# Attention followed by a mixture of experts on one core: the denominators' sums shared between two engines, the seventh batch's routing placed earlier and cut in four

## The chip, the cores and the metric

The kernel runs on one core of a Trainium2 chip. Five engines work side by side: TensorE (PE, matrix products; its weight loads are listed apart as PEld), VectorE (DVE), ScalarE (ACT), GpSimd (POOL) and SyncE (SP), which issues most of the loads. Each engine takes its own instructions strictly in order. The metric is the device time of one execution in microseconds (us).

## The reference

```python
# attention: 8 batches, 12 heads, 448 tokens, 64 wide, float32
scores = cap * tanh(q @ k.T / sqrt(64) / cap)
attn = exp(scores - max);  attn /= sum(attn) + 1e-9
x = (attn @ v), laid out as (3584 tokens, 768)
# experts: 8 of them, 768 -> 1024 -> 768
logits = x @ w_gate + modality_bias[modality_id]
e_idx = argmax(logits);  gate_w = softmax(logits)[e_idx]
out[mask] = gate_w[mask] * (relu(x[mask] @ w1[e]) @ w2[e])   # mask: e_idx == e
```

Each token goes to one expert, so the kernel has to know the expert of every token before it can gather the rows of an expert.

## The kernel before

**Attention.** A group `g` is one pair of heads of one batch: 48 groups (`NG`), six to a batch, and one more turn of the loop (`g = 48`) that finishes the last. In group `g` PE makes the scores of group `g` in four steps (L451; steps 0 and 1 first, then the work of step 1, then steps 2 and 3, then the work of step 3). ACT takes the tanh (`th`, L453) and the exp (`pt`, and `sh` for the step that both heads share, L455). While it does so, PE weighs the values of group `g - 1`: `weigh_own` (L460) with the six parts `pt`, `weigh_shared` (L465) with `sh`, both into the PSUM tile `xT`, of which there is one buffer; DVE copies it out (L588). DVE also prepares the next group's keys and queries as a rounded part `hi` and a rest `lo` (`prep`, L439 and L440), and adds the six `pt` parts into two (`tot`, L557 and L558), for the denominators.

**Sums.** For every three groups (a half batch, `h`), `sums` makes four parts on PE into the tile `glog` (L475). Parts 0 and 1 sum `tot` over the keys, part 2 sums `sh`, part 3 multiplies the unnormalised values `xT` by the gate's weights; `gl` copies the result (L479). Parts 0 and 1 run in one group, parts 2 and 3 in the next. The half batch 13, the last one of the seventh batch (`SOON`), has its four parts in one group, 43. `by_token` turns the result round (`lt`, L487), `logits` divides (L492, L495), `rows_out` transposes the values themselves and scales them (L505, L506) into `xs`, and `store` sends these to device memory (`xd`, L515).

**Routing.** When a batch has its logits, `route` picks the expert of each token on DVE (L210 to L234). At the next group's step 3 it ranks the tokens with two small products on PE (L238, L240), computes rows on DVE, and scatters four lists with indirect DMAs from POOL's queue (`mapd`, L264).

**The first expert slot begins before the last batch is routed.** After the seventh batch, `early_slot` (L284 to L300) counts the tokens of each expert so far and picks one that surely fills a slot of 384 rows. Its result `emeta` gives the address of the rows: POOL loads the list (`mt`, L681) and gathers the rows (`xg`, L688), and SP loads the expert's first weights (`raw`, 18 tiles for the slot of which 6 are `w1`; L88 is the helper of all loads on SP) once DVE's small copy `when` (L610) has handed over the expert's number. `SPLITS` and `MOVES` say at which group and step a weight tile is split into a rounded part `ah` and a rest `al` (L704 on ACT, L705 on DVE) and at which one 128 columns of the gathered rows are transposed (`ptr`, L725) and split in the same way (`x`, L732 to L735).

**Experts.** `ffn1` makes eight blocks of hidden units (`ph`, L752 to L756, 18 products each), `ffn2` the output (`py`, L781). Between the blocks of the first slot stand the last batch's remaining sums, logits, routing and the plan of all later slots. From there on PE is busy with products without a pause worth the name until the last slots.

**What sets the order.** `pin` holds an instruction to the order in which the program is written, on its engine. What is not pinned is placed by a scheduler; `rows_out` on PE, the DVE adds and the SP loads are pinned, and so are the gathers; the stores, the scatters and the small steps of the routing are not.

## Time and profile before

| | |
|---|---|
| median of 3 runs | 955.42 us (949.41 to 956.46) |
| the profiled execution's own time | 955.9 us, span 954.0 us |
| PE busy | 906.7 us, 95% of the span |
| ACT busy | 558.8 us, 59% |
| DVE busy | 549.2 us, 58% |
| POOL busy | 129.7 us, 14% |
| attention, with what of the first slot lies in it | up to 420 us |
| one batch in the middle of the attention | 48.38 us |

A timeline row is: start, duration, engine, line, operation, output and inputs, how many instructions are merged in the row, and in brackets the idle time of the engine ahead of it with what ended that. A group row is: line, engine, operation, shapes and count, then the busy time with the mean of one in ns, then the idle time ahead of it. A window row is: stretch, its length, then for PE, PEld, DVE, ACT and POOL the busy time with the count of instructions, then the TensorE clock granted (1.00 is full speed), the mean busy share of the DMA engines and GB/s. An 'x12' on PE in fp32 is six products, since each takes two passes.

### The profile page before, as it was taken

The page shows a single profiled execution, that of the slowest core. Times are in us where ns is not written, and L with a number is a line of the kernel's source. Part 1 is how long each engine was busy: PE and PEld are TensorE (multiplying, and loading weights), DVE is VectorE, ACT ScalarE, POOL GpSimd, SP SyncE. Part 2 cuts the span into 40 slices and gives each one's busy share as a digit, 9 for nine tenths or more (in the row PEclk, how much of TensorE's full clock was granted, in tenths as well). Part 3 has the DMA queues.
Part 4 walks back from the last instruction along what each step waited for, and adds up shares of the span by engine and source line. Part 5 has one row for each costly group of instructions (what it writes and reads, how often), then busy time and mean ns, then how long its engine had stood idle before and what let it go on. Part 6 is the DMA issues. An engine that isn't in the chain of part 4 may idle for free. (4 is left out here: it accounts for less than half of the span.)

```text
span 954.0 us, 14504 instructions
## 1 busy us (share of the span) xinstructions
PE 906.7 (95%) x5360; PEld 699.8 (73%) x5360; DVE 549.2 (58%) x941; ACT 558.8 (59%) x759; POOL 129.7 (14%) x145
## 2 busy tenths in 40 slices
PE   8999999999999998489999999999999999999986
PEld 3444545454545445258899999999999999988986
DVE  4777777777777778276544443433434444427752
ACT  5998888888888887451544443433434444435551
POOL 2002020202020202102410202020200102010000
PEclk9999999999999999699999999999999999999998
DMA  3433444453436345632773535353454646237560
GB/s 120 119 101 110 134 116 134 115 133 116 127 122 124 125 124 97 197 132 81 259 245 127 197 134 185 126 176 150 161 204 144 221 127 217 81 130 252 197 203 6
DMA packets 47178, 140.01 MB, mean 147 GB/s; under 512 B 8686, under 2 KB 9198, under 8 KB 47088
## 3 DMA queue, kind: packets, MB, share of 16 engines
q1 hardware_dynamic: 38000, 105.78, 36.0%
q0 software_dynamic: 8944, 33.10, 10.4%
q8 instruction: 47, 0.77, 0.4%
q14 instruction: 43, 0.35, 0.1%
q10 hardware_dynamic: 144, 0.00, 0.0%
HBM read 117.35 MB, written 22.69 MB: 147 GB/s over the span
## 5 line engine op out<-in xcount | busy, mean ns | idle before, releaser
L453 ACT ACTIVATE th<-sc,isc 128x896 f32<-128x896 f32 x192 | 168.5, 906 | 68.1 <-PE sc L451 67.9
L756 PE MATMUL ph<-x,al 128*128 128x384 f32 (+2 forms) x528 | 167.7, 318 | 0.0
L781 PE MATMUL py<-bh,hh 128*128 128x384 f32 x464 | 158.7, 343 | 1.5 <-ACT hh L762 1.5
L781 PE MATMUL py<-bh,hl 128*128 128x384 f32 x464 | 156.5, 337 | 0.0
L781 PE MATMUL py<-bl,hh 128*128 128x384 f32 x464 | 156.2, 337 | 0.0
L455 ACT ACTIVATE pt<-th,cabs 128x896 f32<-128x896 f32 x144 | 149.5, 1043 | 2.7
L752 PE MATMUL ph<-x,ah 128*128 128x384 f32 x384 | 129.8, 338 | 4.0 <-DVE x L735 2.6
L753 PE MATMUL ph<-x,ah 128*128 128x384 f32 x384 | 129.4, 337 | 0.0
L460 PE MATMUL xT<-pt,va 128*64 128x448 f32 x576 | 122.0, 560 | 7.3 <-DVE xT L588 7.0
L705 DVE TENSOR_TENSOR bl<-raw,bh 128x768 fp32r<-128x768 f32 x88 | 81.2, 955 | 51.9 <-ACT bh L704 51.6
L704 ACT CAST bh<-raw 128x768 fp32r<-128x768 f32 x88 | 70.3, 840 | 60.1 <-DMA raw<-in_w_dram 54.8
L756 PEld LDWEIGHTS ph<-x,al 128*128 128x128 f32 x528 | 101.5, 192 | 0.0
L705 DVE TENSOR_TENSOR al<-raw,ah 128x1024 fp32r<-128x1024 f32 x66 | 78.8, 1222 | 27.7 <-ACT ah L704 27.4
L762 ACT ACTIVATE hh<-ph 128x384 fp32r<-128x384 f32 x64 | 30.5, 488 | 109.4 <-PE ph L756 104.9
L451 PEld LDWEIGHTS sc<-hi 64*128 64x128 f32 (+1 forms) x336 | 36.9, 189 | 76.3 <-ACT th L453 24.7
L786 ACT ACTIVATE ot<-py,mt 128x384 f32<-128x384 f32 x58 | 33.7, 581 | 98.3 <-PE py L781 49.7
L451 PE MATMUL sc<-hi 64*128 64x448 f32 (+1 forms) x336 | 88.0, 452 | 1.5 <-ACT th L453 0.8
L460 PEld LDWEIGHTS xT<-pt,va 128*64 128x64 f32 x576 | 38.0, 139 | 69.6 <-issue 46.4
L781 PEld LDWEIGHTS py<-bh,hh 128*128 128x128 f32 x464 | 87.1, 188 | 1.9 <-ACT hh L762 1.9
L781 PEld LDWEIGHTS py<-bl,hh 128*128 128x128 f32 x464 | 87.2, 188 | 0.3 <-DVE bl L705 0.2
L781 PEld LDWEIGHTS py<-bh,hl 128*128 128x128 f32 x464 | 87.2, 188 | 0.1
L791 POOL DMA_INDIRECT out_dram<-ot,mt x29 | 32.2, 1109 | 390.5 <-ACT ot L786 310.7
(160 smaller groups left out, 1352.9 us busy)
## 6 DMA issues: line engine op xcount, KB each, us to landing
raw<-in_w_dram SPq DMA_DIRECT2D x66, 512.0 KB, 4.7
raw<-in_w_dram SPq DMA_DIRECT2D x88, 384.0 KB, 4.8
kq<-in_kq_dram SPq DMA_DIRECT2D x47, 480.0 KB, 3.5
va<-in_v_dram SPq DMA_DIRECT2D x48, 256.0 KB, 2.7
xd<-xs POOLq DMA_DIRECT2D x16, 672.0 KB, 5.3
mapd<-pay,pos POOLq DMA_INDIRECT x32, 5.5
xg<-xd,mt POOLq DMA_INDIRECT x30, 5.9
out_dram<-ot,mt POOLq DMA_INDIRECT x29, 4.8
```

Of the source, the lines that this page charges most:

```text
L451: pin(pe.matmul(sc[:, j, :S], k[rows, ks], q[rows, KC2:], start=i == 0, stop=i == 2))
L453: nc.scalar.activation(th[:, :n], sc[:, :n, :S], AF.Tanh, scale=self.isc)
L455: nc.scalar.activation(dst, th[:, :n] if step < KU else th[:, 0], AF.Exp, scale=self.cabs)
L460: pin(pe.matmul(xT[j * D : (j + 1) * D, :S], va[:, u * D : (u + 1) * D], pt[:, u], start=u < 2, stop=False))
L704: a = self.nc.scalar.copy(hi, raw)
L705: b = self.nc.vector.tensor_tensor(lo, raw, hi, op=ALU.subtract)
L752: nc.tensor.matmul(ph[:, :w], hi[:, fs], self.x[:, k, 0, :w], start=first, stop=False)
L753: nc.tensor.matmul(ph[:, :w], hi[:, fs], self.x[:, k, 1, :w], start=False, stop=False)
L756: nc.tensor.matmul(ph[:, :w], lo[:, fs], self.x[:, k, 0, :w], start=False, stop=last)
L781: nc.tensor.matmul(py[:, :HALF], self.h[a][:, f, rows], self.w2s[f][c][:, cs], start=i == 0, stop=i == 3 * FC - 1,)
L786: nc.scalar.mul(ot[:, cs], py[:, :HALF], mt[:, t, 1:2])
L791: nc.gpsimd.indirect_dma_start(self.out, bass.IndirectOffsetOnAxis(ap=mt.bitcast(I32)[:, t, 0:1], axis=0), ot, None, bounds_check=NT - 1, ...
```

## The change

- `sums` loses its part for `sh`. Instead POOL adds `sh` into `tot`: two adds of 64 partitions x 448 for each group (`add`), after DVE's two. The part with the gate's weights comes first now (part 0, in the first of the two groups), and the two parts on `tot` follow in the next. For `g = 47` and `48` the adds of DVE and POOL are put off until after the attention's loop.
- `route` pauses at three places instead of one. For the first six batches its four parts run in four groups. For the last two batches three parts run at once. The fourth of the seventh batch stands, with `early_slot` behind it, at step 1 of group 44 instead of step 3, ahead of the next `prep`.
- `weigh_own` is written ahead of `prep` and the adds.
- The seventh batch's last store goes out on SP's queue, in program order, ahead of the loads of group 47; POOL's queue issued it before.
- All six `w1` tiles of the first slot are loaded at once: four into the staging buffers, two into the buffers of `kq`, made wider for that.
- Splits and transposes of the first slot stand later: nothing of it in group 46; the first two tiles are rounded by DVE (`busy`) instead of ACT.
- In the first slot the rest `bl` of the first four `w2` tiles is subtracted by POOL instead of DVE.
- Two constants become smaller: `pick`, and `ones`, which the warming products at the start read 384 columns wide instead of 512.

```diff
+        yield
...
+        yield
...
-        kq = pool.tile([128, QK], F32, name="kq")
+        kq = pool.tile([128, FF], F32, name="kq")[:, :QK]
...
+            def add(tot, ppt, psh):
+                pin(nc.vector.tensor_tensor(tot, ppt[:, 0:2], ppt[:, 2:4], op=ALU.add))
+                pin(nc.vector.tensor_tensor(tot, tot, ppt[:, 4:6], op=ALU.add))
+                for j in range(2):
+                    rows = slice(j * KR, (j + 1) * KR)
+                    nc.gpsimd.tensor_tensor(tot[rows, j], tot[rows, j], psh[rows], op=ALU.add)
             def weigh_shared(xT, sh, va):
...
                 for t in range(HB):
-                    xs_, tot, sh = kept[h * HB + t]
-                    w = self.pick[:, part] if part < 3 else self.wgt[:, (h * HB + t) % NP]
-                    rhs = (tot[:, 0], tot[:, 1], sh, xs_)[part]
-                    pin(pe.matmul(self.glog[t * GW : (t + 1) * GW, :S], w, rhs, start=part == 0, stop=part == 3))
+                    xs_, tot = kept[h * HB + t]
+                    w = self.pick[:, part - 1] if part else self.wgt[:, (h * HB + t) % NP]
+                    rhs = (xs_, tot[:, 0], tot[:, 1])[part]
+                    pin(pe.matmul(self.glog[t * GW : (t + 1) * GW, :S], w, rhs, start=part == 0, stop=part == 2))
...
-            def store(h, xs):
+            def store(h, xs, queue=nc.gpsimd):
                 b, h0 = divmod(h, NH)
-                nc.gpsimd.dma_start(
+                keep = pin if queue is nc.sync else (lambda inst: inst)
+                keep(queue.dma_start(
                     self.xd[b * S : (b + 1) * S, h0 * HB * 128 : (h0 + 1) * HB * 128].rearrange("(p c) f -> p c f", c=C),
                     xs,
-                )
-            SPLITS = {
-                (NG - 2, 3): (0,),
-                (NG - 1, 1): (1,),
-                (NG - 1, 3): (2,),
-                (NG, 0): (3,),
-                (NG, 2): (4,),
-                (NG, 3): (5,),
-            }
-            MOVES = {(NG - 2, 3): (0,), (NG - 1, 3): (1,), (NG, 1): (2, 3), (NG, 2): (4,), (NG, 3): (5,)}
+                ))
+            SPLITS = {(NG - 1, 1): (0,), (NG - 1, 2): (1,), (NG - 1, 3): (2,), (NG, 0): (3,), (NG, 2): (4,), (NG, 3): (5,)}
+            MOVES = {(NG - 1, 3): (0,), (NG, 1): (1, 2), (NG, 2): (3, 4), (NG, 3): (5,)}
...
             fetch(1)
-            kept, lgs, recs, routing, raws = {}, {}, {}, {}, []
+            adds = []
+            kept, lgs, recs, routing = {}, {}, {}, []
             for g in range(NG + 1):
...
                     if step == 1:
+                        if g:
+                            ppt, psh, pva = pend
+                            xT = ps_x.tile([128, 512], F32, name="xT")
+                            weigh_own(xT, ppt, pva)
+                        if g == NP * (B - 1) + 2:
+                            for way in routing:
+                                next(way, None)
+                            meta = self.early_slot(self.cpool, self.ps_r)
                         if g + 1 < NG:
...
                         if g:
-                            ppt, psh, pva = pend
                             tot = xp.tile([128, 2, S], F32, name="tot", bufs=HB + 2)
-                            pin(nc.vector.tensor_tensor(tot, ppt[:, 0:2], ppt[:, 2:4], op=ALU.add))
-                            pin(nc.vector.tensor_tensor(tot, tot, ppt[:, 4:6], op=ALU.add))
-                            xT = ps_x.tile([128, 512], F32, name="xT")
-                            weigh_own(xT, ppt, pva)
+                            adds.append((tot, ppt, psh))
+                            if g < NG - 1:
+                                add(*adds.pop())
...
                             h, r = divmod(g - HB - 1, HB)
-                            parts = {0: (0, 1), 1: (2, 3), 2: ()}[r] if h != SOON else () if r else range(4)
+                            parts = {0: (0,), 1: (1, 2), 2: ()}[r] if h != SOON else () if r else range(3)
                             for part in parts:
                                 sums(h, part)
-                            if 3 in parts:
+                            if 2 in parts:
                                 gl = copy_sums()
                     if step == 3:
-                        if g in routing:
-                            next(routing.pop(g), None)
+                        for way in routing:
+                            next(way, None)
                         if g == 3:
...
                             self.gate_bias()
-                        if g == NP * (B - 1) + 2:
-                            meta = self.early_slot(self.cpool, self.ps_r)
                         for i, p in enumerate(ROWS.get(g, ())):
...
                             if t == HB - 1:
-                                store(h, xs)
+                                store(h, xs, nc.sync if h == SOON else nc.gpsimd)
                         if g:
...
                             pin(nc.vector.tensor_copy(xs_, xT[:, :S]))
-                            kept[g - 1] = xs_, tot, psh
+                            kept[g - 1] = xs_, tot
                         fetch(g + 2)
...
                                 way = self.route(b, lgs[b], rp, self.ps_r)
-                                next(way)
-                                routing[g + 1] = way
+                                for _ in range(1 if b < B - 2 else 3):
+                                    next(way)
+                                routing = [way]
                     for k in SPLITS.get((g, step), ()):
-                        self.split_w(raws[k], self.w1s[k], pin=True)
-                        if len(raws) < KC:
-                            raws.append(self.load_raw(e, self.w1, len(raws), FF))
+                        self.split_w(raws[k], self.w1s[k], pin=True, busy=k < 2)
                     for k in MOVES.get((g, step), ()):
-                        early_ps = {2: (ps_s, "sc"), 3: (ps_s, "sc"), 5: (self.ps_r, "small")}
-                        self.transpose(k, *early_ps.get(k, (ps_v, "tp")), busy=k < 2, pin=True)
+                        early_ps = {0: (ps_v, "tp"), 3: (ps_v, "tp"), 4: (self.ps_r, "small")}
+                        self.transpose(k, *early_ps.get(k, (ps_s, "sc")), busy=k < 1, pin=True)
                     if (g, step) == (NG - 2, 1):
...
                         e = self.expert(when, 0)
-                        raws = [self.load_raw(e, self.w1, k, FF) for k in range(self.nstage)]
+                        raws = []
+                        for k in range(KC):
+                            raws.append(self.load_raw(e, self.w1, k, FF, None if k < self.nstage else qk.tile([128, FF], F32, name="kq")))
                 if g < NG:
...
                     self.gather(maps, known=NT - S)
+            for pair in adds:
+                add(*pair)
             self.raws = [self.load_raw(e, self.w2, k, DM) for k in range(self.nstage)]
...
             def last_sums():
-                for part in range(4):
+                for part in range(3):
                     sums(NH * B - 1, part, self.ps_y, "py")
...
                 self.way = self.route(B - 1, lgs[B - 1], rp, self.ps_r)
-                next(self.way)
+                for _ in range(3):
+                    next(self.way)
...
-    def load_raw(self, e, src, k, width):
-        raw = self.stg.tile([128, FF], F32, name="raw")
+    def load_raw(self, e, src, k, width, dst=None):
+        raw = self.stg.tile([128, FF], F32, name="raw") if dst is None else dst
         self.load(
...
-    def split_w(self, raw, dst, pin=False):
+    def split_w(self, raw, dst, pin=False, busy=False, minus=None):
         hi, lo = dst
-        a = self.nc.scalar.copy(hi, raw)
-        b = self.nc.vector.tensor_tensor(lo, raw, hi, op=ALU.subtract)
-        if pin:
-            self.pin(a)
-            self.pin(b)
+        keep = self.pin if pin else (lambda inst: inst)
+        keep((self.nc.vector.tensor_copy if busy else self.nc.scalar.copy)(hi, raw))
+        (keep if minus is None else (lambda inst: inst))((minus or self.nc.vector).tensor_tensor(lo, raw, hi, op=ALU.subtract))
...
-    def load_w2(self, e, raws=(), ks=range(FC)):
+    def load_w2(self, e, raws=(), ks=range(FC), minus=None):
         for k in ks:
             raw = raws[k] if k < len(raws) else self.load_raw(e, self.w2, k, DM)
-            self.split_w(raw, self.w2s[k], pin=bool(raws))
+            self.split_w(raw, self.w2s[k], pin=bool(raws), minus=minus)
...
         if n == TW:
-            self.load_w2(cur[0], raws, range(FC // 2 if between else FC))
+            self.load_w2(cur[0], raws, range(FC // 2 if between else FC), self.nc.gpsimd if between else None)
         nxt = ahead() if ahead and not between else None
```

POOL and SP around the gather of the first slot. On POOL before, from the seventh batch's scatter on (`emeta` is the early slot's address, `mt` its list, `xd<-xs` a store, `xg` the gather):

```order
L264 DMA mapd<-pay,pos 31104x2 x4
L94 TENSOR_LOAD emeta
L94 ISA x2
L681 ISA
L681 DMA mt<-mapd 128x6
L255 IOTA pay 112x4
L515 DMA xd<-xs 448x1x384
L688 DMA xg<-xd,mt 128x768 x3
```

On POOL now, from the same scatter on:

```order
L265 DMA mapd<-pay,pos 31104x2 x4
L94 TENSOR_LOAD emeta
L94 ISA x2
L693 ISA
L693 DMA mt<-mapd 128x6
L256 IOTA pay 112x4
L470 TENSOR_TENSOR tot<-tot,sh 64x448 x4
L700 DMA xg<-xd,mt 128x768 x3
L470 TENSOR_TENSOR tot<-tot,sh 64x448 x6
```

The store is gone from between the list and the gather, and four adds (those of groups 44 and 45) stand there. On SP the store stands now as follows, with the loads of groups 46 and 47 around it:

```order
L88 DMA kq<-in_kq_dram 128x960
L88 DMA va<-in_v_dram 128x512
L524 DMA xd<-xs 448x1x384
L88 DMA kq<-in_kq_dram 128x960
L88 DMA va<-in_v_dram 128x512
L96 TENSOR_LOAD when
```

The `kq` load of group 47, its `va` load and the read of `when` are behind the store.

PE at the end of the attention, before, from the end of group 46 (its `xT<-sh,va`) on:

```order
L465 MATMUL xT<-sh,va 128x448
L725 MATMUL ptr<-identr,xg 128x128 x3
L451 MATMUL sc<-hi 128x448 x2
L451 MATMUL sc<-hi,lo 128x448 x2
L451 MATMUL sc<-lo,hi 128x448 x2
L451 MATMUL sc<-hi 128x448 x2
L451 MATMUL sc<-hi,lo 128x448 x2
L451 MATMUL sc<-lo,hi 128x448 x2
L460 MATMUL xT<-pt,va 64x448 x6
L475 MATMUL glog<-sh,pick 32x448 x3
```

And now, from the end of group 47 on, where the first transposes stand:

```order
L473 MATMUL xT<-sh,va 128x448
L495 MATMUL lt<-ident,gl 112x96 x4
L736 MATMUL ptr<-identr,xg 128x128 x3
L461 MATMUL xT<-pt,va 64x448 x6
L736 MATMUL ptr<-identr,xg 128x128 x12
L473 MATMUL xT<-sh,va 128x448
L736 MATMUL ptr<-identr,xg 128x128 x3
```

The three transposes that stood ahead of group 47's scores stand behind the whole of group 47.

DVE at the same place, before, from the copy of group 46's `xT` on (`al` is a weight tile's rest, `x` the split of the gathered rows):

```order
L588 COPY xT<-xT 128x448
L705 TENSOR_TENSOR al_150<-raw,ah_149 128x1024
L732 CAST x<-ptr 128x384
L735 TENSOR_TENSOR x<-ptr,x 128x384
L557 TENSOR_TENSOR tot<-pt 128x896
L558 TENSOR_TENSOR tot<-tot,pt 128x896
L479 COPY gl<-glog 96x448
L705 TENSOR_TENSOR al_152<-raw,ah_151 128x1024
L588 COPY xT<-xT 128x448
```

And now, from the same copy on:

```order
L595 COPY xT<-xT 128x448
L487 COPY gl<-glog 96x448
L718 CAST ah_147<-raw 128x1024
L719 TENSOR_TENSOR al_148<-raw,ah_147 128x1024
L718 CAST ah_149<-raw 128x1024
L500 RECIPROCAL rec<-lt 112x24
L719 TENSOR_TENSOR al_150<-raw,ah_149 128x1024
L595 COPY xT<-xT 128x448
```

The copy of group 47's `xT`, for which PE's next `weigh_own` waits, stands behind both splits of the first two tiles; the two adds `tot` of that group are gone from here and stand behind the last split.

7 lines of the change are left out of this document (3 added, 4 removed).

## The prediction

> **What bounds the kernel now.** I read the windows first, by whole batches of the attention (columns: PE, PEld, DVE, ACT, POOL busy, granted clock, DMA share, GB/s), then 10 us at a time where the attention ends.
>
> ```profile
> 91.52:139.90 48.38, 47.21 (x294) 23.87 (x293) 36.27 (x63) 41.49 (x50) 6.48 (x8) 1.00 0.40 123
> 285.05:333.44 48.39, 47.22 (x295) 23.87 (x294) 36.27 (x63) 41.54 (x50) 6.70 (x8) 1.00 0.49 123
> ...
> 380.00:390.00 10.00, 6.53 (x37) 2.52 (x35) 3.91 (x5) 6.85 (x8) 1.44 (x3) 0.96 0.87 175
> 390.00:400.00 10.00, 0.85 (x3) 0.51 (x3) 1.23 (x1) 1.04 (x1) 3.23 (x3) 0.50 0.83 301
> 400.00:410.00 10.00, 10.00 (x46) 4.63 (x47) 4.58 (x6) 5.33 (x6) 0.00 (x0) 0.68 0.01 2
> ```
>
> A batch takes 48.38 us, of which PE is busy 47.2: PE sets the pace. ACT has 6.9 us to spare in a batch and DVE 12.1, or 2.0 in each of its six groups. From 390 to 400 nearly everything stands still, and PE comes out of it at a clock of 0.68. The chain of waits ahead of that, in the timelines of the engines:
>
> ```profile
> 374.31 0.95 POOL L264 DMA_INDIRECT mapd<-pay,pos  x1 [0.30 <-issue]
> 383.29 0.60 POOL L681 DMA_DIRECT2D mt<-mapd  x1 [8.03 <-DMA mapd<-pay,pos]
> 383.99 0.75 POOL L515 DMA_DIRECT2D xd<-xs  x1
> 391.37 1.08 POOL L688 DMA_INDIRECT xg<-xd,mt  x1 [6.62 <-DMA xd<-xs]
> 394.22 1.00 POOL L688 DMA_INDIRECT xg<-xd,mt  x1 [0.30 <-issue]
> ...
> 378.00 0.69 DVE L506 TENSOR_TENSOR xs<-tp,rec 112x512 f32<-112x512 f32 x1 [1.37 <-PE tp L505]
> ...
> 396.35 0.34 PE L725 MATMUL ptr<-identr,xg 128*128 128x128 f32 x1 [9.82 <-DMA xg<-xd,mt]
> 399.86 0.37 PE L725 MATMUL ptr<-identr,xg 128*128 128x128 f32 x1 [0.75 <-DMA xg<-xd,mt]
> ```
>
> The seventh batch's values `xs` are ready at 378.7, but their store waits on POOL behind the list's load, which waits for the scatter. The gather waits 6.6 us for that store, and PE, in order, waits for the gather with all of group 47 behind it, from 386.5 (396.35 - 9.82) to 399.86, where the last of the three transposes starts.
>
> **The change, term by term**, in the profiled execution's time of 955.9 us (0.5 above the median of the runs, 955.42).
>
> *One product fewer.* Group 43 has all four parts in a row:
>
> ```profile
> 353.37 1.71 PE L475 MATMUL glog<-tot,pick 128*32 128x448 f32 x12
> 354.90 0.93 PE L475 MATMUL glog<-sh,pick 128*32 128x448 f32 x6
> 355.65 0.93 PE L475 MATMUL glog<-xT,wgt 128*32 128x448 f32 x6
> 356.51 0.47 PE L451 MATMUL sc<-hi 64*128 64x448 f32 x2
> ```
>
> By their starts the part on `sh` costs 0.75 us. It is made 16 times, each on PE's own path: 16 x 0.75 = -12.0. ACT stays below it: 41.5 against 48.38 - 1.5 = 46.9. That part 0 and the `tot` parts change places within the pair of groups costs nothing: the tile's end is in the same group, and the gate's part needs only the value copied in the group before.
>
> *POOL's adds.* The trace has no such instruction. The nearest rows of POOL, a fill and a table, and for the ports two casts of DVE, one beside the fill and a wider one alone:
>
> ```profile
> 5.54 2.02 POOL L984 MEMSET xg<- 128x2304 f32 x1 [2.36 <-DVE identr L108]
> 5.85 1.98 DVE L439 CAST hi<-kq 128x512 fp32r<-128x512 f32 x1 [0.45 <-issue]
> 10.91 0.66 DVE L439 CAST hi<-kq 128x960 fp32r<-128x960 f32 x1 [1.75 <-DMA kq<-in_kq_dram]
> ...
> L142 POOL IOTA blkj<- 128x80 f32 x1 | 0.3, 307 | 0.0
> ```
>
> By the fill 448 elements cost 448/2304 x 2.02 = 0.39 us, by the table 448/80 x 0.307 = 1.72. I take the middle, 1.0 for one add. [...]
>
> Two adds a group fill 2.0 of some 7.8 us, with 6.5 us a batch of other POOL work: the queue holds. The cast of 512 took 1.98 us beside the fill, against 0.66 for 960 alone, so an operation of POOL can hold DVE for its whole length. Where does it meet DVE? In an ordinary group DVE waits for PE after `tot` (1.37 us in the row at 378.00) and then reads PSUM (`xs`, `xT`); I count nothing there. The place that costs is the group after a batch's logits, where DVE is already late:
>
> ```profile
> 131.43 1.09 DVE L558 TENSOR_TENSOR tot<-tot,pt 128x896 f32<-128x896 f32 x1
> 133.23 0.62 DVE L588 COPY xT<-xT 128x448 f32<-128x448 f32 x1
> 133.90 2.48 PE L460 MATMUL xT<-pt,va 128*64 128x448 f32 x12 [1.17 <-DVE xT L588]
> ...
> PE xT L460 <- DVE xT L588: 7.0, 6, 1.2
> ```
>
> PE waits 1.17 us there for the copy of `xT`, six times, 7.0 us. With the routing in four parts the rows of the rank leave this group, about 0.35 us; but most small steps now stand between `tot` and `xs`, just where the adds run. Free of contention each batch gains 0.35; with both adds fully exposed it loses 2 x 1.72 - 0.35 = 3.1. I take one add exposed, 1.0 - 0.35, and 0.2 for adds that pile up behind the scatter, for which POOL's list waits: +0.85 x 6 = +5, with ends of -2 and +25 (the 3.1, and another 1.1 of piled adds, times six). The sums need these adds two groups later, some 15 us, so PE shouldn't wait for POOL itself.
>
> [...]
>
> *Group 44.* PE waits there for the early slot's count:
>
> ```profile
> PE cps L279 <- DVE rows L244: 2.5, 1, 2.5
> ...
> 372.00 0.63 DVE L588 COPY xT<-xT 128x448 f32<-128x448 f32 x1
> 373.44 2.48 PE L460 MATMUL xT<-pt,va 128*64 128x448 f32 x12
> ```
>
> Of the 2.5 us only 0.8 can be gained: group 45's `weigh_own` at 373.44 needs the copy that ends at 372.63, and that has the same DVE work ahead of it as before. It goes into the next term.
>
> *The end of the attention.* With the store on SP behind `xs`, at 378.7 - 0.8 = 377.9, it lands 6.0 later, at 384; the scatter starts some 4 us earlier, since the rank now stands ahead of a `prep` and two adds on DVE (0.65 for `hi`, about 1.1 for each of the others), so the list is there too. The gather is issued behind POOL's adds at about 385 to 388.5 and lands 5.6 later, by 394. PE no longer asks for it until the end of group 47, at about 394. So this wait goes. What is late next is the first expert's weights:
>
> ```profile
> kq<-in_kq_dram SPq DMA_DIRECT2D x2, 480.0 KB, 3.9
> xd<-xs POOLq DMA_DIRECT2D x2, 672.0 KB, 6.0
> xg<-xd,mt POOLq DMA_INDIRECT x3, 5.6
> ...
> 379.30 0.65 DVE L439 CAST hi<-kq 128x960 fp32r<-128x960 f32 x1
> 383.26 0.13 DVE L610 COPY when<-emeta 1x1 int32<-1x1 int32 x1
> 384.53 75.59 SPq L88 DMA_DIRECT2D raw<-in_w_dram  x18
> 390.72 1.04 ACT L704 CAST ah<-raw 128x1024 fp32r<-128x1024 f32 x1 [2.68 <-DMA raw<-in_w_dram]
> 391.80 1.23 DVE L705 TENSOR_TENSOR al<-raw,ah 128x1024 fp32r<-128x1024 f32 x1 [4.60 <-ACT ah L704]
> 400.85 0.56 DVE L735 TENSOR_TENSOR x<-ptr,x 128x384 fp32r<-128x384 f32 x1
> 428.90 0.94 PE L475 MATMUL glog<-tot,pick 128*32 128x448 f32 x2
> ...
> 450.42 0.34 PE L756 MATMUL ph<-x,al 128*128 128x384 f32 x1
> 453.54 0.34 PE L756 MATMUL ph<-x,al 128*128 128x384 f32 x1
> ```
>
> On SP the store stands ahead of group 47's `kq`, which is thus issued at 378 and lands 3.9 later, at 381.9. Its `hi` was at 379.30: DVE, `when` behind it, and the weights on SP slip by 2.6. The first raw tile, 6.2 us after its issue before, comes at 390.72 + 2.6 = 393.3. From there DVE has the whole slot's splits in one row: six `al` at 1.2, two casts at 0.7, six `x` rests at 0.56 and one `x` cast, two copies of `xT` and the small steps of the logits, 14 us: the last `x` at about 407.5. All six weight tiles are issued at once, 3.1 MB, at the 300 GB/s of the window 10 us: they stay ahead. PE ends its first block 0.2 later, then eight transposes of `xT` (0.8) and the second block (18 products, 453.54 - 450.42 = 3.1), so that the next row, the sums of the last half batch, comes at 411.8. Before it came at 428.90: -17.1. I give back 2 for products at the lower clock after a thin stretch. -15, with ends of -6 (the weights 6 us later, or the clock down throughout) and -18 (no slip on SP).
>
> *The adds put off.* The last `tot` ends 4.4 us behind the last `x`, and POOL's two adds behind that: about 413.8, where PE wants them at 413.4: +0.4, ends 0 and 3. The `w2` rests on POOL are needed only by `ffn2`, behind eight blocks of 3.1 us, and the smaller constants lie in a wait for the first load: nothing.
>
> Sum: -12.0 + 5 - 15 + 0.4 = -21.6, so **934 us**.
>
> **The rivals.** *The adds cost nothing* (they fit in DVE's waits, and the routing's wait shrinks): -12 - 2 - 17 = -31, 925. For it: DVE's 2 us a group. Against: the cast of 1.98. *The end of the attention doesn't shorten*: a later link, the weights or the gather, takes up most of the wait: 955.9 - 12 + 5 - 5 = 944. For it: the 2.6 us on SP and a DMA share of 0.87; against: 17 us are a lot to lose. *POOL becomes the bound of DVE*, the one that ends slower: if each add takes 1.7 and shuts DVE out for its length in every group, six groups need 36.3 + 6 x 3.4 = 56.9 us of DVE in a batch of 48.38, +8.5 x 7.5 batches = +64, less 15: about 1005. It decides once the two adds together exceed DVE's free time, now (46.9 - 36.3)/6 = 1.8 us, and fall on its work rather than on its waits. Against it: in ordinary groups they fall on reads of PSUM. *ACT paces the attention instead* and the product's 12 us don't show: 946; but ACT has 5 us a batch left.
>
> **The numbers.** Forecast, 926 to 942: 0.62. Adds free: 0.10. End not shorter: 0.13. ACT: 0.04. A contention beyond my upper guess that only eats the gain, 942 to 955: 0.05. POOL's bound, or another slip: 0.06. The range from 924 to 947 leaves out 2 in 10. A measurement of this kernel tells about 1% from no change. Faster by over 1% is below 945.9: 0.62 + 0.10 + most of 0.13 and a share of the rest, 0.82. Within 1%: 0.12. Slower: 0.06.
>
> **What would show it.** The batch windows: about 47.7 us instead of 48.38, with 0.75 less for each `sh` part and the wait of `weigh_own` for `xT` at 1.8 us in the routing's group. POOL's adds in groups of lines at about 1.0 us. At the end: no wait of PE for `xg` over 1 us, the `xd` store on SP right behind `xs`, and DVE as the engine that ends last before the first expert block. I'd be wrong if the batch stayed at 48.4 or more, or if PE still stood idle 8 us or more ahead of the first block.

## The result: about 1% slower, where 2% faster was forecast

| | before | after |
|---|---|---|
| median | 952.41 us (947.27 to 956.46, 4 runs) | 965.22 us (957.59 to 968.08, 4 runs) |
| profiled execution, span | 954.0 us | 962.6 us |
| mean granted clock | 0.983 | 0.974 |

The ratio of after to before is 1.0116, with a 95% interval of 1.0074 to 1.0159. The forecast was 934 us, with 947 at the upper end of its range.

Two places of the program cut the profiled execution into three stretches: `weigh_shared` of group 43, the last one that the new end of the attention doesn't touch, and the first product of the last half batch's sums, where the first expert slot is under way. The rows of both places, of before (one row), of after (two rows); the second one of before, at 428.90, stands in the prediction.

```profile
358.91 0.92 PE L465 MATMUL xT<-sh,va 128*128 128x448 f32 x2
```
```profile
368.37 0.92 PE L473 MATMUL xT<-sh,va 128*128 128x448 f32 x2
435.55 0.94 PE L483 MATMUL glog<-xT,wgt 128*32 128x448 f32 x2
```

| stretch | before | after | difference | forecast |
|---|---|---|---|---|
| start to group 43 | 358.91 | 368.37 | +9.5 | -5.5 (14 of 16 products at 0.75, and +5 for POOL's adds) |
| group 43 to the last half batch's sums | 69.99 | 67.18 | -2.8 | about -16 |
| from there to the end | 525.1 | 527.05 | +2.0 | +0.4 |

So the miss of 30 us has two halves. The batches became longer by nine where they should have become shorter by five, and the end of the attention gave 3 us in place of 16.

**The batches.** The windows of after (columns as in the prediction: PE, PEld, DVE, ACT, POOL busy, clock, DMA share, GB/s), two batches, the stretch of a routing group, and the end of the attention:

```profile
82.59:132.31 49.72, 47.19 (x283) 23.85 (x281) 38.57 (x64) 41.59 (x50) 20.56 (x19) 0.97 0.47 117
284.18:332.52 48.34, 45.89 (x282) 23.38 (x281) 38.16 (x64) 41.46 (x50) 20.61 (x19) 1.00 0.50 124
...
86.60:92.00 5.40, 4.69 (x18) 1.30 (x18) 4.48 (x6) 2.37 (x3) 0.61 (x1) 0.68 0.28 91
...
390.00:400.00 10.00, 7.41 (x41) 3.46 (x39) 4.56 (x6) 7.08 (x9) 8.35 (x8) 0.87 0.79 227
400.00:410.00 10.00, 9.06 (x42) 3.61 (x42) 3.70 (x6) 5.07 (x8) 1.72 (x2) 0.79 0.81 294
410.00:420.00 10.00, 6.16 (x29) 2.98 (x29) 8.15 (x14) 4.53 (x8) 0.00 (x0) 0.83 0.03 4
420.00:430.00 10.00, 4.62 (x14) 4.62 (x15) 6.65 (x7) 1.42 (x2) 2.31 (x2) 0.57 0.59 209
```

PE's busy time did fall, from 47.22 to 45.89 in the second batch: the product is gone. But a batch still takes 48.3 to 51.6 us; the five between 82.59 and 332.52 take 49.99 in the mean. Most of the idle time has one place, the routing's group. The change was to spread the routing's four parts over four groups; on DVE most of the second part, the third and the first steps of the fourth (`gs`), which aren't pinned, run together in one, in each of these batches. DVE and POOL there in after, then PE:

```profile
81.89 1.09 DVE L467 TENSOR_TENSOR tot<-tot,pt 128x896 f32<-128x896 f32 x1
...
83.11 0.19 DVE L226 TENSOR_REDUCE first<-sc 112x4 f32<-112x32 f32 x1
83.22 1.12 DVE L261 TENSOR_SCALAR gs<-gs 112x4 f32<-112x4 f32 x1
84.25 0.18 DVE L228 TENSOR_TENSOR oh<-sc,first 112x32 bf16<-112x32 f32 x1
...
84.46 1.46 DVE L234 TENSOR_TENSOR before<-before,oh 112x8 bf16<-112x8 bf16 x3
...
86.65 0.61 DVE L595 COPY xT<-xT 128x448 f32<-128x448 f32 x1
...
83.17 2.34 POOL L470 TENSOR_TENSOR tot<-tot,sh 64x448 f32<-64x448 f32 x2 [5.42 <-DVE gs L260]
...
87.31 3.90 PE L461 MATMUL xT<-pt,va 128*64 128x448 f32 x12 [2.39 <-DVE xT L595]
...
PE xT L461 <- DVE xT L595: 23.3, 13, 2.8
```

POOL's two adds take 2.34 us. A `TENSOR_SCALAR` on 112x4 numbers that DVE starts just after the first one takes 1.12 us, until that add is over; three little adds take 1.46 us across the second. The copy of `xT` is late by what they lost, PE waits 2.39 us for it (1.17 before), and `weigh_own` behind this wait runs at a clock of 0.68 (from 86.60 to 92.00) and takes 3.90 us in place of 2.48. That wait was 7.0 us over the execution, all in the six routing groups; it is 23.3 now, 15.0 of it there.

**The end of the attention.** The waits in the timelines of SP, DVE, PE and ACT in after:

```profile
388.55 0.67 SPq L524 DMA_DIRECT2D xd<-xs  x1
389.27 0.81 SPq L88 DMA_DIRECT2D kq<-in_kq_dram  x1
...
400.50 2.14 SPq L88 DMA_DIRECT2D raw<-in_w_dram  x4
402.92 16.33 SPq L88 DMA_DIRECT2D kq<-in_w_dram  x2
...
395.17 0.73 DVE L440 CAST hi<-kq 128x960 fp32r<-128x960 f32 x1 [6.11 <-DMA kq<-in_kq_dram]
424.77 0.55 DVE L746 TENSOR_TENSOR x<-ptr,x 128x384 fp32r<-128x384 f32 x1
...
422.55 1.04 ACT L718 CAST ah<-kq 128x1024 fp32r<-128x1024 f32 x1 [4.16 <-DMA kq<-in_w_dram]
...
399.93 4.60 PE L461 MATMUL xT<-pt,va 128*64 128x448 f32 x12 [0.75 <-DVE xT L595]
411.43 3.97 PE L461 MATMUL xT<-pt,va 128*64 128x448 f32 x12 [2.37 <-DVE lg L503]
425.38 0.69 PE L763 MATMUL ph<-x,ah 128*128 128x384 f32 x1 [7.79 <-DVE x L746]
```

The wait of 9.82 us for the gather is gone, as forecast. Others took its place. Group 47's `kq` goes out behind the store, and DVE waits 6.11 us for it. The group `kq x2` on SP hides a gap: the fifth weight tile is issued at 402.92, the sixth only at 418.92, since both go through one buffer and the sixth waits for the split of the fifth. Its split on ACT waits 4.16 us for the landing, the last `x` ends at 425.3, and PE has by then stood still for 7.79 us. And through all this PE runs at clocks of 0.57 to 0.87.

### The profile page after: what moved, and what is told of

It is laid out like the page before. It is cut to its first block, busy times and chain, and to the rows that moved or that the text cites. A ratio compares the mean times of both kernels' runs of the same rounds, so it can differ in the third digit from the quotient of the medians.

```text
span 962.6 us, 14524 instructions
## 1 busy us (share of the span) xinstructions
PE 905.7 (94%) x5264; PEld 701.1 (73%) x5264; DVE 564.9 (59%) x936; ACT 558.0 (58%) x758; POOL 252.9 (26%) x244
## 3 DMA queue, kind: packets, MB, share of 16 engines
q0 software_dynamic: 8768, 32.42, 10.2%
## 5 line engine op out<-in xcount | busy, mean ns | idle before, releaser
L470 POOL TENSOR_TENSOR tot<-tot,sh 64x448 f32<-64x448 f32 x96 | 113.7, 1184 | 228.2 <-DVE tot L467 148.0
L461 PE MATMUL xT<-pt,va 128*64 128x448 f32 x576 | 130.5, 592 | 25.9 <-DVE xT L595 23.3
L719 DVE TENSOR_TENSOR bl<-raw,bh 128x768 fp32r<-128x768 f32 x84 | 77.6, 954 | 48.6 <-ACT bh L718 47.0
L797 ACT ACTIVATE ot<-py,mt 128x384 f32<-128x384 f32 x58 | 33.7, 581 | 101.2 <-PE py L792 55.3
L719 DVE TENSOR_TENSOR al<-raw,ah 128x1024 fp32r<-128x1024 f32 x64 | 76.3, 1220 | 23.3 <-ACT ah L718 23.2
```

Of the source, the lines that this page charges most:

```text
L461: pin(pe.matmul(xT[j * D : (j + 1) * D, :S], va[:, u * D : (u + 1) * D], pt[:, u], start=u < 2, stop=False))
L470: nc.gpsimd.tensor_tensor(tot[rows, j], tot[rows, j], psh[rows], op=ALU.add)
L719: (keep if minus is None else (lambda inst: inst))((minus or self.nc.vector).tensor_tensor(lo, raw, hi, op=ALU.subtract))
L797: nc.scalar.mul(ot[:, cs], py[:, :HALF], mt[:, t, 1:2])
```

## The experiments

Two theories for the batches: POOL's adds hold DVE up (theory 1), or cutting the routing in four does it without POOL (theory 2). One for the end: the single buffer and the store ahead of the last keys (theory 3). What the expectations call the port theory is theory 1 in a narrower form: an add holds operations of DVE up for the time in which it runs. The runs show the longer times (a `TENSOR_SCALAR` of 1.12 us in place of 0.16); what in the chip brings them isn't shown. In the table a period is the mean of the five batches that lie, in after, between the `weigh_shared` at 82.59 and the one at 332.52, the group ahead of the routing's; the last three columns are the three stretches from above.

| run | median us | ratio to before (95%) | period | to group 43 | to the sums | to the end |
|---|---|---|---|---|---|---|
| before | 953.5 | | 48.38 | 358.91 | 69.99 | 525.1 |
| after | 965.22 | 1.0116 (1.0074 to 1.0159) | 49.99 | 368.37 | 67.18 | 527.1 |
| no_adds | 943.67 | 0.9885 (0.983 to 0.994) | 47.26 | 348.41 | 64.69 | 528.4 |
| short_adds | 942.87 | 0.9883 (0.9828 to 0.9939) | 47.04 | 349.66 | 65.25 | 524.5 |
| one_route | 964.68 | 1.0098 (1.0061 to 1.0136) | 50.44 | 370.95 | 64.66 | 526.7 |
| mixed_adds | 954.18 | 0.9993 (0.9958 to 1.0027) | 48.07 | 358.59 | 65.92 | 525.6 |
| route_behind | 944.98 | 0.9907 (0.9876 to 0.9937) | 48.22 | 360.00 | 67.81 | 523.7 |
| sums_pe | 949.30 | 0.9954 (0.9932 to 0.9975) | 48.29 | 358.93 | 63.18 | 520.2 |
| sums_pe_six | 948.04 | 0.9915 (0.987 to 0.9961) | 48.70 | 359.56 | 64.73 | 522.8 |
| sums_pe_six_late | 945.62 | 0.9897 (0.9863 to 0.9931) | 48.91 | 362.38 | 57.88 | 519.2 |
| two_kq_late | 981.92 | 1.0284 (1.0233 to 1.0335) | 53.36 | 391.13 | 64.60 | 526.6 |
| sums_pe_two_late | 960.64 | 1.0065 (1.0032 to 1.0098) | 50.90 | 375.27 | 57.15 | 523.6 |
| route_behind_six_late | 946.03 | 0.9927 (0.99 to 0.9954) | 48.08 | 357.30 | 63.69 | 523.6 |
| route_behind_six | 945.98 | 0.9917 (0.9886 to 0.9949) | 47.77 | 355.45 | 63.81 | 524.9 |

Where the denominators lack the shared unit, other experts can be chosen, so for no_adds and short_adds the stretches up to group 43 are the clean comparison.

The periods and stretches come from one execution of each run, and executions of one kernel differ by some 10 us: the one of sums_pe is the fastest of its ten (943.85), that of sums_pe_six_late the second fastest of seven (941.18), that of route_behind the slowest of its ten (953.31). The next table divides the way to group 43 in these executions: when the first `weigh_shared` (group 1) starts, what the six routing groups and all others up to group 43 take from one `weigh_shared` to the next, and how long PE waits in each kind (waits over 0.3 us, in sum).

| run | group 1 starts | six routing groups | the others | PE waits, routing | PE waits, others |
|---|---|---|---|---|---|
| before | 23.07 | 57.0 | 278.9 | 7.0 | 0 |
| after | 23.70 | 66.9 | 277.7 | 15.0 | 4.8 |
| no_adds | 21.04 | 50.1 | 277.3 | 4.5 | 4.0 |
| short_adds | 23.06 | 50.5 | 276.1 | 5.0 | 2.0 |
| one_route | 23.04 | 55.9 | 292.0 | 10.4 | 12.0 |
| mixed_adds | 22.71 | 52.5 | 283.4 | 7.0 | 9.0 |
| route_behind | 23.24 | 45.1 | 291.7 | 0 | 13.7 |
| sums_pe | 23.23 | 54.2 | 281.5 | 4.2 | 2.2 |

### Without the adds (no_adds)

```diff
-                    nc.gpsimd.tensor_tensor(tot[rows, j], tot[rows, j], psh[rows], op=ALU.add)
```

> The changed kernel without the two additions of the shared unit's weights on POOL; the denominators lack the shared unit, so part of the computation is left out (the products, the routing in four parts and the end of the attention stay as they are in the changed kernel). Theory 1, the additions on POOL hold DVE back and with it the copy of xT that weigh_own waits for: the batches fall from 49.7 us (mean of the five periods between 82.59 and 332.52 in the trace of after: 49.99) to 46.9 to 47.3, which is the 48.38 of before less two products of 0.75 us; weigh_shared of group 43 comes at 345 to 351 instead of 368.37; DVE's tensor_scalar of the routing falls from 1119 ns back to about 165 ns; PE's wait for xT falls from 23.3 us to under 9; the time is 18 to 25 us under the changed kernel's. Theory 2, the routing in four parts does it by itself, without POOL: the period stays at 49 us or more and the time within 6 us of the changed kernel's.

Measured: 943.67 us, 21.6 under after; period 47.26, group 43 at 348.41, the routing's `TENSOR_SCALAR` at 162 ns in the mean. Theory 1's numbers, but for the wait for `xT` of 11.6 us, which was to fall below 9. The same place of the program in this run, DVE and PE:

```profile
79.08 0.16 DVE L261 TENSOR_SCALAR gs<-gs 112x4 f32<-112x4 f32 x1
...
79.42 0.56 DVE L234 TENSOR_TENSOR before<-before,oh 112x8 bf16<-112x8 bf16 x3
...
81.37 2.48 PE L461 MATMUL xT<-pt,va 128*64 128x448 f32 x12 [0.61 <-DVE xT L592]
...
348.41 0.92 PE L470 MATMUL xT<-sh,va 128*128 128x448 f32 x2
```

1.12 us became 0.16, 1.46 became 0.56, the wait 0.61, and `weigh_own` takes 2.48 us. Group 43 comes 10.50 us earlier than before, and 14 products at 0.75 make 10.5. That the two agree to the tenth is luck: 2.0 of the 10.50 were won ahead of group 1, where the first `weigh_own` took 2.48 us in this execution and 3.88 in that of before; PE waits 2.5 us less in the routing groups and 4.0 more in the others. Without these the products make 10.0. POOL's adds cost 368.37 - 348.41 = 20.0 us up to group 43, 17.3 from group 1 on, and 16.9 of these lie in the six routing groups: 10.4 us of waits, and 5.9 us by which `weigh_own` was slower after them.

### Adds over a seventh of the columns (short_adds)

Taking the adds away also takes away their waits and their places in POOL's queue. This run keeps these and shortens the work.

```diff
-                    nc.gpsimd.tensor_tensor(tot[rows, j], tot[rows, j], psh[rows], op=ALU.add)
+                    nc.gpsimd.tensor_tensor(tot[rows, j, :64], tot[rows, j, :64], psh[rows, :64], op=ALU.add)
```

> The changed kernel with the additions on POOL kept where they are, as many, with the same waits, but over 64 columns in place of 448; the other 384 columns of the denominators lack the shared unit, so part of the computation is left out. If it is the time in which POOL works that holds DVE's small operations back (the port theory): an addition takes 0.15 to 0.4 us, the routing group falls from 11.4 us to 8.2 to 9.0, the period from 49.99 to 47.0 to 48.0, and the time is 14 to 22 us under the changed kernel's, near the run without additions (943.67). If it is the order in POOL's queue (additions that wait for tot standing ahead of the stores and the scatter) or the waits between the engines: the period stays above 49 and the time within 6 us of the changed kernel's.

Measured: 942.87 us, period 47.04, routing groups of 8.3 to 8.7 us. The group rows of POOL's adds and of the `TENSOR_SCALAR`, first in after, then in this run:

```profile
L470 POOL TENSOR_TENSOR tot<-tot,sh 64x448 f32<-64x448 f32 x96 | 113.7, 1184 | 228.2 <-DVE tot L467 148.0 <-DVE gs L260 25.9 <-DMA mapd<-pay,pos 25.5
L261 DVE TENSOR_SCALAR gs<-gs 112x4 f32<-112x4 f32 x8 | 7.0, 880 | 0.0
```
```profile
L470 POOL TENSOR_TENSOR tot<-tot,sh 64x64 f32<-64x64 f32 x96 | 33.0, 344 | 260.4 <-DVE tot L467 161.7 <-DMA mapd<-pay,pos 35.2 <-DVE sc L222 33.3
L261 DVE TENSOR_SCALAR gs<-gs 112x4 f32<-112x4 f32 x8 | 2.0, 256 | 0.0
```

(In after six of the eight `TENSOR_SCALAR` were held for 1.1 us, the other two took 0.16.) As many adds, with the same waits, cost nothing that can be measured against none at all. It is the time in which POOL works, not the number of adds or their places in its queue.

### The routing cut once (one_route)

```diff
             nc.vector.tensor_tensor(L, L, bias[:, ds(b, 1)].rearrange("p o c e -> p (o c) e"), op=ALU.add)
-        yield
...
-        yield
         before = pool.tile([CP, C, E], BF16, name="before")
...
-                                for _ in range(1 if b < B - 2 else 3):
+                                for _ in range(1):
```

> The changed kernel with the routing cut only once, as before (the additions on POOL stay). Theory 1 (POOL's additions): the period stays at 49 to 50.5 us, PE's wait for xT stays above 18 us, and the time is within 6 us of the changed kernel's, since the additions still fall on DVE's work of the routing group. Theory 2 (the order of the routing's parts): the period returns to 48.4 or below, and the time falls by 10 us or more.

Measured: 964.68 us, period 50.44, wait for `xT` 26.5 us. The time is that of after, so theory 2 falls. But the loss has moved, against what was expected: the routing groups take 9.3 us (9.5 before, 11.2 in after), and the `TENSOR_SCALAR` 164 ns. Instead three other groups take 11.2 to 13.7 us. In the longest one the adds, late behind the scatter, stand ahead of the store of `xs` on POOL, and DVE waits for that store before it can write the next `xs`; POOL, DVE and PE:

```profile
103.43 3.77 POOL L468 TENSOR_TENSOR tot<-tot,sh 64x448 f32<-64x448 f32 x2
107.14 0.73 POOL L522 DMA_DIRECT2D xd<-xs  x1
...
112.78 0.69 DVE L512 TENSOR_TENSOR xs<-tp,rec 112x512 f32<-112x512 f32 x1 [3.44 <-DMA xd<-xs]
...
114.06 4.75 PE L459 MATMUL xT<-pt,va 128*64 128x448 f32 x12 [3.40 <-DVE xT L593]
```

Under both orders the time is the same, but it is lost in different places.

### One group's adds on DVE (mixed_adds)

```diff
-                    nc.gpsimd.tensor_tensor(tot[rows, j], tot[rows, j], psh[rows], op=ALU.add)
+                    (pin if busy else (lambda i: i))((nc.vector if busy else nc.gpsimd).tensor_tensor(tot[rows, j], tot[rows, j], psh[rows], op=ALU.add))
...
-                                add(*adds.pop())
+                                add(*adds.pop(), busy=g > NP and g % NP == 3)
```

> The changed kernel with the additions of one group in six, the one in which DVE works out the batch's routing, on DVE in place of POOL; the others stay on POOL. Port theory: only that group was held, so its step falls from 11.4 us to 8.4 to 9.6 (8.2 without additions, and two additions of about 0.6 us on DVE), the period from 49.99 to 47.2 to 48.6, DVE's tensor_scalar of the routing from 1119 ns to about 165, and the time is 8 to 16 us under the changed kernel's: 949 to 957. If additions beside the other groups' preparations cost as much: the time is within 6 us of the changed kernel's.

Measured: 954.18 us, 11.0 under after; period 48.07, routing groups of 8.6 to 8.8 us. Group 43 comes at 358.59, about half way from 368.37 to 348.41. The routing groups give back 14.4 of their 16.9 us. The other groups became 5.6 longer in sum than in after, where POOL's adds cost them next to nothing (277.7 against 277.3 without adds), and PE waits 9.0 us in them in place of 4.8. How much of that the two adds on DVE cost isn't shown.

### The routing behind the copy of xT (route_behind)

The adds stay on POOL, and DVE does first what others wait for: each part of the routing is held behind `moved`, the copy of that group's `xT`.

```diff
-                        for way in routing:
-                            next(way, None)
...
-                            pin(nc.vector.tensor_copy(xs_, xT[:, :S]))
+                            moved = pin(nc.vector.tensor_copy(xs_, xT[:, :S]))
                             kept[g - 1] = xs_, tot
+                            with tc.issue_after(moved.ins):
+                                for way in routing:
+                                    next(way, None)
```

> The changed kernel, additions on POOL unchanged, but each part of the routing stands on DVE behind the copy of that group's xT in place of ahead of it. Port theory: the additions then still hold the routing's small operations up, but nobody waits for those; PE's waits for xT fall from 23.3 us to under 12, the routing group's step from 11.4 us to 8.2 to 9.5, the period from 49.99 to 47.2 to 48.5, and the time is 8 to 18 us under the changed kernel's: 947 to 957. Against it: if what follows on DVE (the next preparation, hi and lo) is then late instead and PE waits for that, the step stays above 10.5 us and the time within 5 us.

Measured: 944.98 us, ratio 0.9907 (0.9876 to 0.9937): 20 us under after and faster than before, below the range that was expected. The same group here, on DVE, POOL and PE:

```profile
84.24 0.68 DVE L514 TENSOR_TENSOR xs<-tp,rec 112x512 f32<-112x512 f32 x1
84.85 0.62 DVE L593 COPY xT<-xT 128x448 f32<-128x448 f32 x1
85.39 0.18 DVE L217 TENSOR_REDUCE mx<-L 112x4 f32<-112x32 f32 x1
...
85.83 1.09 DVE L222 SCALAR_TENSOR_TENSOR sc<-L,desc 112x32 f32<-112x32 f32 x1
...
84.51 2.36 POOL L470 TENSOR_TENSOR tot<-tot,sh 64x448 f32<-64x448 f32 x2 [5.46 <-DVE tot L467]
...
86.17 2.48 PE L461 MATMUL xT<-pt,va 128*64 128x448 f32 x12
```

The adds still hold an operation of the routing up (`sc`, 1.09 us), but PE no longer waits for it: the group takes 7.5 us (11.4 in after, 8.2 without adds). The routing's second, third and fourth part now also stand in three groups (on DVE from 85.4, 93.9 and 101.2 us on), so that the run changes two things at once: behind the copy, and spread out. In this execution the six routing groups win 21.8 us, and the others give back 13.9 (PE waits 13.7 us in them). Single groups of 9.5 to 12.2 us are left; in the longest one an add that waited for the scatter falls on a preparation.

### The sums on PE again (sums_pe)

```diff
-                    nc.gpsimd.tensor_tensor(tot[rows, j], tot[rows, j], psh[rows], op=ALU.add)
...
-                    rhs = (xs_, tot[:, 0], tot[:, 1])[part]
+                    rhs = (tot[:, 0], tot[:, 1], sh, xs_)[part]
...
-                            parts = {0: (0,), 1: (1, 2), 2: ()}[r] if h != SOON else () if r else range(3)
+                            parts = {0: (0, 1), 1: (2, 3), 2: ()}[r] if h != SOON else () if r else range(4)
```

> The changed kernel with the denominators' sums as before: the shared unit's weights are added by a fourth product on PE, nothing on POOL; routing in four parts and the new end of the attention stay. Theory 1: the period is 48.2 to 48.6 us, weigh_shared of group 43 comes at 357 to 360, and what is left against the kernel before is the end of the attention alone; there the trace of after took 67.2 us from weigh_shared of group 43 to the sums of the last half batch against 70.0 before, so the time is 0 to 8 us under the kernel before. Theory 2 (routing in four parts slows the batches): the period is 49 us or more and the time at or over the kernel before's.

Measured: 949.30 us, 4.2 under before. Group 43 comes at 358.93, 0.02 from before, so that the stretch behind it is the new end of the attention by itself: 63.18 us to the sums against 69.99, 6.8 us gained in this execution. It is shorter by another 4.9 us behind the sums, which isn't explained; the medians differ by 4.2 in all. PE stands still for 8.0 us ahead of the first expert block here too.

### The sixth tile and the late store (sums_pe_six, sums_pe_six_late)

Both on top of sums_pe. The buffer of the first keys stays allocated and idle throughout the attention; the sixth tile goes there. In the second run the store stands behind `fetch` as well.

```diff
-                            raws.append(self.load_raw(e, self.w1, k, FF, None if k < self.nstage else qk.tile([128, FF], F32, name="kq")))
+                            raws.append(self.load_raw(e, self.w1, k, FF, None if k < self.nstage else self.first if k == KC - 1 else qk.tile([128, FF], F32, name="kq")))
...
-                            if t == HB - 1:
-                                store(h, xs, nc.sync if h == SOON else nc.gpsimd)
+                            if t == HB - 1 and h != SOON:
+                                store(h, xs)
...
                         fetch(g + 2)
+                        if NP * (B - 1) + 9 - 6 <= g == max(ROWS):
+                            store(SOON, xs, nc.sync)
```

> The changed kernel with the sums on PE as before (nothing on POOL), and the sixth weight tile loaded into the buffer of the first keys and queries, which is idle by then, in place of the one that the fifth holds. Theory 3, the sixth tile's late load sets the start of the expert blocks: PE's wait ahead of the first block falls from 8.0 us to 3.5 to 5, ACT's wait of 4.4 us for that load goes, the sums of the last half batch come 3 to 5 us earlier after the weigh_shared of group 43 than the 63.2 us of the run with the sums on PE, and the time falls by 3 to 5 us against it (949.3): 944 to 947. Its rival, that the splits and transposes on ACT and DVE end as late anyway: the wait stays above 7 us, the time within 1.5 us.

> As the run before it, and SP's store of the seventh batch's rows stands behind the loads of that group's keys in place of ahead of them. If the last keys behind the store cost PE time: DVE's wait of 6.2 us for them goes, the steps of groups 45 and 46 (11.2 and 7.8 us) shorten by 2 to 4 us, and the time falls by 2 to 4 us more: 941 to 945. If that wait is covered by other work: under 1 us either way; if the store's delay then makes the gather late, PE's wait for xg comes back (13.0 us before the change) and the time rises by 3 us or more.

Measured: 948.04 and 945.62 us, both just above what was expected. The wait ahead of the first block fell from 8.0 to 4.4 and 4.2 us, as theory 3 has it. But with the sixth tile alone the stretch to the sums didn't shorten (64.73 against 63.18), against what was expected. PE has nearly the same short waits there in both runs (0.59 and 1.50 us; 0.50, 0.63 and 1.50); in one the clock holds, in the other it doesn't. The windows after these waits, and `weigh_own`, in sums_pe, then in sums_pe_six:

```profile
391.00:397.00 6.00, 5.91 (x34) 2.52 (x35) 1.74 (x4) 2.74 (x3) 0.00 (x0) 1.00 0.82 261
...
391.09 2.48 PE L462 MATMUL xT<-pt,va 128*64 128x448 f32 x12 [1.50 <-DVE xT L593]
```
```profile
392.00:401.00 9.00, 8.64 (x34) 3.06 (x35) 1.84 (x4) 2.85 (x4) 0.00 (x0) 0.65 0.85 284
...
392.36 4.75 PE L465 MATMUL xT<-pt,va 128*64 128x448 f32 x12 [1.50 <-DVE xT L596]
```

The clock took back 3.6 us there (group 47's step is 13.8 us against 10.2). With the late store the waits for `kq` and `hi` go, that step is 7.8 us, and the stretch falls to 57.88: 12.1 under before. Theory 3 holds for the waits; in the medians both repairs together are worth 3.7 us, and the sixth tile alone can't be told from sums_pe.

### Keys loaded a group ahead (two_kq_late, sums_pe_two_late)

All keys and queries in two buffers in turn, which the fifth and sixth weight tile then use too, and the late store; once on after, once with the sums on PE.

```diff
-        kq = pool.tile([128, FF], F32, name="kq")[:, :QK]
+        if g < 2:
+            self.kqs = getattr(self, "kqs", []) + [pool.tile([128, FF], F32, name="kq")]
+        kq = self.kqs[g % 2][:, :QK]
```

> The changed kernel with the keys and queries loaded into two buffers in turn (the first one is used again, where only one rotated), which the fifth and sixth weight tiles then share too, and with SP's store of the seventh batch's rows behind the loads of that group. Theory 3, the gain at the end of the attention is lost because the sixth weight tile waits for the split of the fifth and the last keys stand behind the store: the sixth tile is issued by 405 instead of 418.92, the last x is split 5 to 8 us earlier and PE's wait of 7.8 us ahead of the first expert block falls below 2; DVE's waits for kq (13.9 us in 50 to 350) fall below 3 and the period by 0.3 to 1 us; the time falls by 8 to 15 us. Its rival, that ACT's and DVE's own splits and transposes set that end: the wait ahead of the first expert block stays above 5 us and the time falls by less than 4.

> As the run with the sums on PE, the sixth tile and the late store, but with two buffers in turn for all keys and queries, so that these are loaded a group ahead. In the changed kernel that made the batches longer (periods of 50 to 56 us). If the early loads by themselves do it, sharing the DMA engines with the store of xs that DVE waits for: landing of the stores takes 7 us or more against 5 to 6, the period is 49 to 52 us against 48.3, and the time 5 us or more over 945.62. If it takes both, the early loads and POOL's additions: the period is 48.0 to 48.6 and the time within 3 us of 945.62.

Measured: 981.92 us, 17 over after where 8 to 15 under was expected, the plainest miss of the study; and 960.64 us, 15 over sums_pe_six_late. The sixth tile goes out within 1 us of the fifth, and the wait ahead of the first block falls to 4.4 us in both (below 2 was expected), but the batches grew to 53.4 and 50.9 us, the second without any add on POOL: the early loads do it by themselves. The group of the scatter in two_kq_late, on SP, POOL and DVE:

```profile
211.63 0.39 SPq L88 DMA_DIRECT2D kq<-in_kq_dram  x1
...
211.52 0.72 POOL L526 DMA_DIRECT2D xd<-xs  x1 [1.60 <-DVE pos L252]
...
223.26 0.69 DVE L516 TENSOR_TENSOR xs<-tp,rec 112x512 f32<-112x512 f32 x1 [6.79 <-DMA xd<-xs]
```

The load now goes out at the same time as the store of `xs`. The next `xs` is written into the one buffer that this store reads, and DVE waits 6.79 us for it, `xT` and PE behind. With one buffer the load goes out only after the next preparation, 2.8 us behind the store in the same group of sums_pe_six_late. The stores up to 380 us landed after 7.3 us in the median in sums_pe_two_late, against 5.6 in sums_pe; around one scatter, with two stores in each run, it was 8.3 us, against 6.1 in sums_pe_six_late. That load and store delay each other when they move at once is the author's estimate from these times; it wasn't tried apart.

### The repairs together (route_behind_six_late, route_behind_six)

> The run before it, with the sixth weight tile in the idle buffer of the first keys and the store behind the loads of the last keys. Both were worth 3.7 us together where the sums stay on PE (945.62 against 949.3); here the same: 3 to 6 us under the run before it. If POOL's put-off additions of the last groups hold the end of the attention up: less than 2 us.

> The run with the routing behind the copies of xT, with the sixth weight tile in the idle buffer and the store left where the change put it, ahead of the last keys. If the late store took back what the sixth tile gave (PE waited 5.8 us for xg in the run with both): PE's wait for xg is 2 to 3 us, its wait ahead of the first expert block 4.4 us, and the time 2 to 5 us under the run with the routing behind alone (944.98): 940 to 943. If the end of the attention gives nothing there because the later stages wait anyway: 944 to 947.

Measured: 946.03 and 945.98 us, no better than route_behind alone (944.98), against what was expected of the first. With the late store PE waits 5.8 us for `xg` again; without it the wait is gone and the time is the same. Where the 4 us of the shorter end go there stays open. None of the best four runs (944.98 to 946.03) can be told from the others.

## Why the prediction was wrong

- **"One product fewer", -12.0: right.** 10.0 us for 14 products up to group 43, forecast 10.5, once the luckier start and the changed waits of no_adds are taken out.
- **"POOL's adds", +5 with ends of -2 and +25: mis-sized, and the first step that failed.** The term took 1.2 us a routing group for the adds, 7.2 in all six; they cost 16.9 there, which would have made it about +15. One add's price was right (1.0 forecast; 1.18 in the mean, 1.14 undisturbed), the place was right (the routing's group), and so was the way it costs: an operation of DVE beside an add takes longer (1.12 us in place of 0.16 for the `TENSOR_SCALAR`). What failed is "I take one add exposed": 1.8 of the 2.34 us were in the first of these groups (a wait of 2.39 us for `xT` against 0.61 without adds), 1.7 in the mean. And one cost wasn't in the term: after four of the six waits, of 2.4 to 2.8 us, `weigh_own` took 3.6 to 4.2 us in place of 2.48, 5.9 us together; after the other two it took 2.48. More than the `TENSOR_SCALAR` is held in after: beside an add `lo` takes 1.98 us in place of 1.16, and the first of the two adds of `tot` on DVE 2.04 in place of 1.08, three times each up to 420 us.
- **The other groups: a term put at nothing.** PE didn't wait at all in them before; it waits 4.8 us in after, and 2.0 to 4.0 in no_adds, short_adds and sums_pe, so the adds aren't the cause. DVE has waits that it hardly had before: up to 360 us, in no_adds, 13.3 us for the store of `xs` and 19.9 for keys (none and 5.9 before). What in the new order brings them isn't shown. These 4.8 us, 0.6 ahead of group 1 and the 9.7 by which the adds were mis-sized make up the 15 us by which the batches missed.
- **"POOL becomes the bound of DVE", the slower rival: not what happened.** DVE's busy time went from 36.3 to 38.4 us a batch, far from 56.9. The kernel became slower by the forecast's own mechanism, between its middle and its upper end, joined by a shortfall elsewhere; as forecast, ordinary groups absorb their adds in this order. That reads of PSUM aren't held was the author's assumption, which no row of before shows; in after they keep their times beside an add: `xT` takes 0.62 us (16 copies beside one, 26 without one up to 420 us), `xs` 0.69 (12 and 19).
- **"The end of the attention", -15 with ends of -6 and -18: -2.8 in after, -6.8 in the execution of sums_pe.** Right: the gather's wait goes. Wrong, first: "they stay ahead". "All six weight tiles are issued at once" isn't what the program does: five are, and the sixth goes out 16 us later, for the two buffers of `kq` are only one, the other being held by the first keys; that cost PE 3.6 us (8.0 to 4.4). Wrong, second: "PE ends its first block 0.2 later". The first product waits for the last `x`, and the block then runs at a low clock (0.57 from 420 to 430 in after). From the last `x` to the sums it is 9.0 us in sums_pe (413.0 to 422.1), where the forecast had 4.3; before it was the same 8.9, from this row to 428.90:

```profile
420.00 0.69 PE L752 MATMUL ph<-x,ah 128*128 128x384 f32 x1 [2.65 <-DVE x L735]
```

  In sums_pe, with group 43 where it was before, the last `x` comes at 413.0 (forecast 407.5) and what follows is 4.7 longer: 10.2 us, and the gain of 17.1 fell short by 10.3. Underrated, third: the store ahead of the keys of group 47, forecast as a slip of 2.6 us, made DVE wait 6.1 to 6.7 us in after, sums_pe and sums_pe_six, and PE fall into short waits after which the clock was low in some executions (0.65 in that of sums_pe_six) and not in others (1.00 in that of sums_pe).
- **"The adds put off", +0.4:** they ran from 427.62 to 433.85, ahead of the last sums, which start at 435.55; nothing was lost there. The further 2.0 us behind the sums aren't explained; that stretch varies by as much between kernels that are alike in it (523.6 to 527.1 us with all adds on POOL).
- **The signs named beforehand** worked. The wait of `weigh_own` was to be 1.8 us and is 2.4 to 2.8; a batch of 48.4 or more, and a stop of some 8 us ahead of the first block, were to mean a wrong forecast, and both came.

## What to carry to other kernels

Work moved to GpSimd is not free because GpSimd is idle: look up what VectorE does in the same microseconds, and put what others wait for ahead of it. Here the adds cost 17 us with small operations ahead of the awaited copy, and the kernel became 20 us faster when these stood behind it; what the adds cost there by themselves wasn't measured. Work that a scheduler may move doesn't run where it is written: read from the trace in which group it runs. Before a load is counted as issued, count the buffers that really rotate. And a load that is made earlier can collide with whatever is moving then: here, as far as the times tell, it delayed a store that VectorE waited for (7.3 us to the landing in the median in sums_pe_two_late, 5.6 in sums_pe), and the kernel lost more than it was meant to gain.

## What the runs showed of the hardware

- A GpSimd add of 64x448 in fp32 takes 1.14 us in the median in after, one of 64x64 0.34 in the mean in short_adds. Beside it, the VectorE operations of this kernel that read PSUM (`xs` 0.69, `xT` 0.62, `gl` 0.62) and the reduction `mx` (0.18 in route_behind) keep their times; a `TENSOR_SCALAR` of 112x4 takes 1.12 us in place of 0.16, a `SCALAR_TENSOR_TENSOR` of 112x32 1.09 in place of 0.19: both last to the end of the add.
- The granted clock after a short stop of PE isn't the same each time: after nearly the same waits (0.59 and 1.50 us; 0.50, 0.63 and 1.50) it was 1.00 in one execution and 0.65 in another, and `weigh_own` took 2.48 or 4.75 us. In the routing groups of after it took 3.6 to 4.2 us behind four of the six waits of 2.4 to 2.8 us and 2.48 behind the other two. What decides it isn't shown by any run.
- Between kernels that differ only ahead of it, the stretch behind the last half batch's sums differs by some 4 us (519.2 to 523.6 with the sums on PE, 523.6 to 527.1 with all adds on POOL); repairs of 3 to 4 us in the profile can vanish in the median.
